# The first two batches with nine tokens per partition, and their scores ahead of V W_in, in a fused attention and two-layer kernel

## The chip, the cores and the metric

One core of a Trainium2 chip runs the whole program. The metric is the device time of one execution in microseconds, taken as the median of several runs; smaller is better. The engines are TensorE (PE, with its weight loads as PEld), VectorE (DVE), ScalarE (ACT), GpSimd (POOL) and SyncE (SP), which here issues nearly all transfers.

## What is computed

```python
# q, k, v: (8, 8, 576, 64)   phi: (8, 8, 576, 32)     batch, heads, tokens
a = np.exp(phi - phi.max(axis=2, keepdims=True))        # max over tokens
a = a / (a.sum(axis=2, keepdims=True) + 1e-9)
k_m = np.einsum('bhsm,bhsd->bhmd', a, k)                # 32 memories per head
v_m = np.einsum('bhsm,bhsd->bhmd', a, v)
scores = q @ k_m.transpose(0, 1, 3, 2) / np.sqrt(64)
attn = softmax(scores)                                  # with + 1e-9 under the sum
x = (attn @ v_m) -> (4608, 512)
h = x @ moe_w_in                                        # 512 x 2048
x = (h - np.tanh(h)) @ moe_w_out                        # 2048 x 512
h = np.maximum(np.maximum(x @ w1, x @ w2), x @ w3)      # 512 x 768 each
out = h @ moe2_w_out                                    # 768 x 512
```

The weights and all inputs arrive as the reference has them; `moe_w_in`, `moe_w_out` and the later weights come as 64-bit words, which the kernel turns into one or two 32-bit parts on chip (a conversion).

## The kernel before

Attention is not multiplied out: instead of attn @ v_m and then @ w_in, the kernel builds V W_in (the memories times the weights, `vw_gen`, PSUM tiles `ps_w`, SBUF tiles `vw`) per batch and half of the hidden columns, and multiplies the attention weights `at` by it (`ps_h`). Then follow tanh and subtraction (`emit_g`: `th` on ACT and DVE, `gh` in a high part by ACT and a low part by POOL), and the product with w_out (`emit_x`, PSUM tiles `ps_x`, weights `wo`). Every product of split numbers is three matmuls (`mm3`).

Work runs in steps: a step is one token tile times one block of 128 hidden columns. The first four tiles have 288 tokens each (half a batch); tiles 1 and 2 of the program are batch 0, tiles 3 and 4 batch 1. They go through `wo` blocks 0 to 3 first and through 4 to 7 after that. Later tiles have 256 to 512 tokens and all eight blocks at once. After two such phases the second layer runs from line 732 on.

For each batch `phi_gen` takes the maximum over tokens (`mx` on DVE, turned by PE into `ps_mx`, reduced to `mt`, spread by `dg`), subtracts and exponentiates; `kv_mm` multiplies by k and v (`ps_kv`), divides by the sums (`rc`, `n`) and turns the result (`ps_t`) into `kT` and `vT`. `q_gen` transposes the queries in blocks of 32 (`qT`), makes the scores (`sc`), transposes them back (`s`), takes the softmax, and transposes again (`aT`) into `at`, for each half `hf` of a batch.

In all batches tokens lie as 18 per partition of 32 partitions for the queries, and as four per partition of 128 plus a rest of 64 for phi, k and v. A query half of 4 heads takes 8 transfers (line 224), with 128-byte pieces.

A conversion (`conv`) is two ACT passes (`cvb`, `cva`) on a raw tile, three DVE passes on `cvb`, and a POOL addition; w_out needs another ACT cast and another POOL subtraction. There are three `raw` tiles, so a fourth fetch waits until one is converted.

Each engine works its instructions in program order. The order is that in which the Python code issues them, as rearranged by the scheduler of the language; the head of the program (lines 596 to 618) drives generators by hand, and later ones stand in three tracks: `fg` (attention of the next batches), `bg` (conversions) and `ld` (query loads), of which `slot` runs some pieces after every group of matmuls. `need` empties a track up to a named entry when a step wants what it makes.

Of the kernel before, what the change touches and what calls it, by code (L numbers as in the profile page):

```python
# [22 lines left out]
def kernel(  # L23
# [124 lines left out]
    def convs(*jobs, ahead=2):  # L148
        raws, k = [], 0
        for src, hi, lo in jobs:  # L150
# [7 lines left out]
            yield from conv(raws[k - 1], hi, lo)  # L158

    def conv(raw, hi, lo=None):  # L160
# [10 lines left out]
        live[0] -= 1  # L171
# [15 lines left out]
    def wi_conv(fq):  # L187
        t = wo1.tile([P, HP, FQ], F32, name="wi2") if fq == 2 else wi_p.tile([P, HP, FQ], F32, tag="wi", bufs=2, name="wi")
        yield from convs(*((moe_w_in[r * P:(r + 1) * P, fq * FQ:(fq + 1) * FQ], t[:, r], None) for r in range(HP)), ahead=2 if fq else 3)
        wi[fq] = t  # L190


    phi_t, kv_t, q_t = {}, {}, {}

# [99 lines left out]

    def kv_gen(b):
        yield from phi_gen(b)
# [5 lines left out]
    def q_gen(b, hfs):  # L302
        if 0 in hfs:
            ld.need(("q", b, 1))
# [4 lines left out]
        for hf in hfs:  # L309
            qT = []  # L310
            for g in range(2):
                t = ap.tile([P, 2, NH], F32, tag="qT", bufs=2, name="qT")
                V.transpose(out=t, in_=q_t[b, g][:, :, hf * JH:(hf + 1) * JH].rearrange("p r j d -> p r (j d)"))
                qT.append(t)
                yield
            scs = [bank(e, [P, NH], "sc") for e in range(2)]
            small([(scs[e][32 * r:32 * r + 32], kT[b][64 * e:64 * e + 64, r], qT[r // 2][64 * e:64 * e + 64, r % 2])
                   for r in range(HP) for e in range(2)])
# [26 lines left out]
            if hf:  # L345
# [25 lines left out]
    def wo_conv(fcs, p):  # L371
        ts = [p.tile([P, 2, DM], F32R, name=f"wo{fc}") for fc in fcs]
        for k, _ in enumerate(convs(*((moe_w_out[fc * P:(fc + 1) * P, :], t[:, 0], t[:, 1]) for fc, t in zip(fcs, ts)))):
            yield
        for fc, t in zip(fcs, ts):
            wo_t[fc] = t
# [49 lines left out]
    class Track:  # L426
# [6 lines left out]
        def step(self, now):  # L433
            if self.q and self.q[0][2] <= now:
                try:
# [3 lines left out]
                    self.step(now)  # L439

# [136 lines left out]
    G.memset(ones, 1.0)  # L577
    def drain(*gens):
# [17 lines left out]
    load_phi(0)  # L596
    load_kv(0)
    w0 = wi_conv(0)
    next(w0)
    drain(load_q(0, 0))  # L600
    next(w0)
    drain(load_q(0, 1))
    next(w0)
    drain(phi_gen(0))
    drain(kv_mm(0), w0)
    wo0 = wo_conv(range(4), wo_p)
    next(wo0)
    next(wo0)
    load_phi(1, fetch.last)
    load_kv(1, fetch.last)  # L610
    drain(q_gen(0, (0,)))
    drain(vw_gen(0, 0, 0))
    for _ in range(5):
        next(wo0)
    S.mark = at_cast[-1]
    background[0] = True
    drain(q_gen(0, (1,)), part_of(wo0, 6))
    background[0] = False
# [223 lines left out]
    def outs(g):  # L842
# [12 lines left out]
        def done(u):  # L855
            ob = get(f"ob{u % 2}")
            (S.copy if u % 2 else V.tensor_copy)(ob, ps[u])
            for r in range(0, P, 32):
                b, j = divmod((g * NG + u * P + r) // 32, TJ)
                dst = out[b * NS:(b + 1) * NS, :].rearrange("(p j) e -> j p e", j=TJ)  # L860
                DMA.dma_start(out=dst[j], in_=ob[r:r + 32, :])
# [66 lines left out]
```

## Time and profile before

| | us |
|---|---|
| median of 3 runs | 1371.06 |
| lowest, highest | 1369.17, 1372.64 |
| the profiled execution | 1365.75 |
| its span, first to last instruction | 1364.0 |
| PE busy | 1285.4 (94%) |
| PEld busy | 1157.4 (85%) |
| DVE busy | 751.2 (55%) |
| POOL busy | 531.8 (39%) |
| ACT busy | 507.1 (37%) |

Busy times are of one profiled execution. A busy share over the span is a mean over stages that differ; what counts is which engine is busy in the stage that is looked at. In the rows further down, "idle before <- releaser" says how long the engine stood and what ended it.

### The profile page before, as it was taken

The page shows a single profiled execution, that of the slowest core. Times are in us where ns is not written, and L with a number is a line of the kernel's source. Part 1 is how long each engine was busy: PE and PEld are TensorE (multiplying, and loading weights), DVE is VectorE, ACT ScalarE, POOL GpSimd, SP SyncE. Part 2 cuts the span into 40 slices and gives each one's busy share as a digit, 9 for nine tenths or more (in the row PEclk, how much of TensorE's full clock was granted, in tenths as well). Part 3 has the DMA queues.
Part 4 walks back from the last instruction along what each step waited for, and adds up shares of the span by engine and source line. Part 5 has one row for each costly group of instructions (what it writes and reads, how often), then busy time and mean ns, then how long its engine had stood idle before and what let it go on. Part 6 is the DMA issues. An engine that isn't in the chain of part 4 may idle for free.

```text
span 1364.0 us, 22739 instructions
## 1 busy us (share of the span) xinstructions
PE 1285.4 (94%) x8996; PEld 1157.4 (85%) x8996; DVE 751.2 (55%) x1189; ACT 507.1 (37%) x993; POOL 531.8 (39%) x470
## 2 busy tenths in 40 slices
PE   3578898999998999999999999999999999999998
PEld 1457696897897799898989999999999899999996
DVE  3868557666545755756643344555734546457342
ACT  2446244454334455555544332223322323233221
POOL 1637334554423546776754341132311312223110
PEclk9989998999999899999999999999999999999999
DMA  8874847866714536667575139838557477385431
GB/s 204 243 194 127 207 139 189 215 213 172 186 57 178 189 105 236 242 206 251 207 254 168 50 125 364 342 126 307 192 171 286 141 270 268 97 307 197 166 132 47
DMA packets 188394, 264.94 MB, mean 194 GB/s; under 512 B 94976, under 2 KB 160512, under 8 KB 179200
## 3 DMA queue, kind: packets, MB, share of 16 engines
q1 hardware_dynamic: 188000, 259.82, 58.3%
q0 software_dynamic: 288, 3.67, 0.7%
q8 instruction: 71, 1.16, 0.4%
q14 instruction: 35, 0.29, 0.1%
HBM read 199.49 MB, written 63.96 MB: 193 GB/s over the span
## 4 chain that ended last, share of the span: by engine, by line
PE 84%; DVE 7%; SPq 3%; issue 2%; POOL 2%; ACT 1%; DMA 1%; POOLq 0%; ACTq 0%; DVEq 0%
PE b L57 40%; PE ps_x L57 26%; PE ps_h L57 13%; PE ps_w L57 2%; PE ps_kv L57 2%; DVE cvb L57 2%; SPq L224 1%; DVE st L57 1%; DVE s L57 1%; POOL s L57 1%; DVE mx L57 1%; DMA raw<-in_moe_w_out_dram 1%; SPq L214 1%; DVE th L57 1%; DVE vw L57 0%
## 5 line engine op out<-in xcount | busy, mean ns | idle before, releaser
L57 PE MATMUL ps_x<-gh,wo 128*128 128x320 f32 (+2 forms) x2400 | 451.9, 335 | 7.2 <-DVE xo L57 5.5
L57 PEld LDWEIGHTS ps_x<-gh,wo 128*128 128x128 f32 x2400 | 381.4, 191 | 54.7 <-issue 22.9
L57 PE MATMUL b<-mv,sw 128*128 128x384 f32 x2268 | 401.6, 338 | 0.0
L57 PEld LDWEIGHTS b<-mv,sw 128*128 128x128 f32 x2268 | 399.1, 188 | 1.4 <-DMA sw<-sw_d 0.3
L57 POOL TENSOR_TENSOR gh<-th,gh 128x320 fp32r<-128x320 f32 (+2 forms) x200 | 209.8, 1051 | 259.0 <-ACT gh L57 248.9
L57 PE MATMUL ps_h<-at,vw 128*128 128x256 f32 (+2 forms) x1536 | 254.9, 307 | 20.4 <-DVE th L57 10.0
L57 PEld LDWEIGHTS ps_h<-at,vw 128*128 128x128 f32 x1536 | 227.7, 197 | 47.7 <-DVE th L57 15.6
L57 DVE TENSOR_TENSOR th<-ps_h,th 128x320 f32<-128x320 f32 (+2 forms) x200 | 106.7, 536 | 184.2 <-ACT th L57 183.5
L57 ACT ACTIVATE th<-ps_h 128x320 f32<-128x320 f32 (+2 forms) x200 | 95.2, 478 | 200.2 <-PE ps_h L57 185.7
L57 PE MATMUL b<-wz,mh 128*128 128x512 f32 x648 | 150.4, 390 | 1.1 <-DVE ob L57 1.1
L57 PEld LDWEIGHTS b<-wz,mh 128*128 128x128 f32 x648 | 121.3, 188 | 26.5 <-DVE ob L57 2.0
L57 ACT CAST gh<-th 128x320 fp32r<-128x320 f32 (+2 forms) x200 | 99.6, 499 | 96.0 <-DVE th L57 83.8
L57 POOL TENSOR_TENSOR c<-c,u 128x384 f32<-128x384 f32 x36 | 36.5, 1015 | 226.6 <-ACT u L57 226.6
L57 ACT COPY p<-b 128x384 f32<-128x384 f32 x108 | 51.8, 479 | 169.6 <-PE b L57 146.4
L57 DVE TENSOR_TENSOR c<-b,u 128x384 f32<-128x384 f32 x72 | 39.9, 554 | 97.0 <-PE b L57 97.0
L57 DVE TENSOR_SCALAR cvb<-cvb 128x512 f32<-128x512 f32 x112 | 69.8, 624 | 29.8 <-ACT cvb L57 27.0
L57 DVE TENSOR_TENSOR m<-c,m 128x768 f32<-128x768 f32 x72 | 69.0, 958 | 5.7 <-DVE c L57 0.9
L57 DVE TENSOR_TENSOR c<-b,p 128x384 f32<-128x384 f32 x72 | 37.7, 554 | 37.7 <-ACT p L57 34.2
L57 DVE TENSOR_TENSOR vw<-ps_w,vw 128x512 fp32r<-128x512 f32 x64 | 41.4, 681 | 22.9 <-ACT vw L57 22.9
L57 POOL TENSOR_TENSOR mv<-xr,mv 128x384 fp32r<-128x384 f32 x30 | 48.9, 1664 | 12.4 <-PE b L57 9.3
L57 POOL TENSOR_TENSOR m<-m,u 128x384 f32<-128x384 f32 x18 | 21.4, 1189 | 81.6 <-ACT u L57 80.2
L57 ACT CAST mh<-m 128x384 fp32r<-128x384 f32 (+1 forms) x54 | 31.8, 620 | 57.1 <-DVE m L57 57.1
(82 smaller groups left out, 1051.5 us busy)
## 6 DMA issues: line engine op xcount, KB each, us to landing
sw<-sw_d SPq DMA_DIRECT2D x52, 1792.0 KB, 7.6
sw_d<-so SPq DMA_DIRECT2D x9, 1792.0 KB, 7.1
raw<-in_moe_w_out_dram SPq DMA_DIRECT2D x22, 512.0 KB, 5.5
qt<-in_q_dram SPq DMA_DIRECT2D x128, 72.0 KB, 3.1
at_d<-at SPq DMA_DIRECT2D x16, 576.0 KB, 3.7
at<-at_d SPq DMA_DIRECT2D x8, 1152.0 KB, 6.3
raw<-in_moe_w_dram SPq DMA_DIRECT2D x18, 512.0 KB, 4.0
out_dram<-ob SPq DMA_DIRECT2D x144, 64.0 KB, 1.7
```

The source lines that it names most:

```text
L57: i = op(*a, **kw)
L214: DMA.dma_start(out=t[:64, i, :, 4], in_=x[b, :, 4 * P:].rearrange("h p d -> p h d"))
L224: q_dma.dma_start(out=t[64 * e + 32 * h:64 * e + 32 * h + 32, r], in_=src[e, h, r])
```

## The change

Batches 0 and 1 (`b < SPREAD`, with `SPREAD = 2`) get another layout. Partition p holds nine consecutive tokens; an upper and a lower set of 64 partitions hold odd and even heads, so a pair of heads fills 128 partitions. phi, k and v come in one transfer each, the queries of a batch in two, and the queries of both batches are issued at the start, into tiles that are used for other things later (`wo4`, `wo6`, `vw`). `kv_spread` replaces `phi_gen` and `kv_mm` for these batches: maxima and sums are trees of four DVE operations, the 40 one-column matmuls for the sums become two, and k and v take 72 matmuls of 64 rows. The query transposition covers all 576 tokens at once; the halves of a batch are then the upper and lower 32 partitions of each 64, so the scores of a half are two accumulating passes of 32 rows. `kT` is made in two parts to match (`kTs`). The output rows of these batches are written with stride 9.

The order changes as well. Scores of batch 0 stand ahead of V W_in; the second half of batch 0 moves from the head into the track `fg`, behind which `q_gen(1, (0,))` stands ahead of V W_in of batch 1; three w_in loads are issued early, the fourth into a `vw` buffer; a small exponential at the start loads ACT's table; `wo` blocks 4 to 7 are named as soon as each is converted, and `bg.until` runs the track only as far as the wanted block.

```diff
@@ small
-        ins = [T.matmul(o, w, x, start=True, stop=True).ins for o, w, x in mms]
+        ins = [T.matmul(o, w, x, start=not any(t), stop=not t or all(t), skip_group_check=bool(t)).ins for o, w, x, *t in mms]
@@ loads
+    def spread(t, x):
+        return DMA.dma_start(out=t.rearrange("p r j d -> p r (j d)"),
+                             in_=x.rearrange("(r e) n d -> r (e n) d", e=2).rearrange("r (p j) d -> p r (j d)", p=P)).ins
@@ kv_spread
+        mx = tree(V.tensor_max, pc, "mx")
...
+        for c in range(C9):
+            for r in range(HP):
+                for e in range(2):
+                    ins.append(T.matmul(ps[e][32 * r:32 * r + 32, :2 * D], ph[64 * e:64 * e + 64, r, c], t[64 * e:64 * e + 64, :, r, c], start=c == 0, stop=c == C9 - 1, skip_group_check=True).ins)
...
+        part = tree(V.tensor_add, pc, "part")
+        for e in range(2):
+            T.matmul(ps[e][:, 2 * D:], part[64 * e:64 * e + 64], ones[64 * e:64 * e + 64, :1], start=True, stop=True, skip_group_check=True)
@@ q_gen
+                w = [32 * (2 * e + hf) for e in range(2)]
+                small([(scs[e][32 * r:32 * r + 32].rearrange("p (j c) -> p j c", c=32), kT[b][w[e]:w[e] + 32, t, r], qT_s[b, r // 2][w[e]:w[e] + 32, r % 2, t], t)
+                       for t in range(2) for r in range(HP) for e in range(2)])
@@ emit_x
-        while 8 * ph + fc not in wo_t:
-            bg.need("wo")
+        bg.until(lambda: 8 * ph + fc in wo_t)
@@ start
+    S.activation(ap.tile([P, 2], F32, tag="mt", bufs=1, name="warm"), ones[:, :2], AF.Exp)
...
+    drain(kv_gen(0), part_of(w0, 3), part_of(q0, 2))
...
+    drain(q0, w0)
...
     drain(vw_gen(0, 0, 0))
...
+    fg.add(("q", 0, 0), q_gen(0, (1,)))
     fg.add("kv", kv_gen(1))
+    fg.add(("q", 0, 1, 0), q_gen(1, (0,)))
     fg.add(("vw", 0, 1, 0), vw_gen(0, 1, 0))
-    fg.add(("q", 0, 1, 0), q_gen(1, (0,)))
```

On SP, at the start of the program, the transfers stand like this before (`raw` is a tile of w_in or w_out, `qt` queries):

```order
L198 DMA phi<-in_phi_dram 128x8x128
L199 DMA phi<-in_phi_dram 64x8x32
L211 DMA kv<-in_k_dram 128x8x256
L214 DMA kv<-in_k_dram 64x8x64
L211 DMA kv<-in_v_dram 128x8x256
L214 DMA kv<-in_v_dram 64x8x64
L141 DMA raw<-in_moe_w_in_dram 128x1024
L224 DMA qt<-in_q_dram 32x18x32 x8
L141 DMA raw<-in_moe_w_in_dram 128x1024 x2
L224 DMA qt<-in_q_dram 32x18x32 x8
L141 DMA raw<-in_moe_w_in_dram 128x1024
L141 DMA raw<-in_moe_w_out_dram 128x1024
```

And now, where `qs` are the queries of batch 1:

```order
L211 DMA phi<-in_phi_dram 128x4x288
L211 DMA kv<-in_k_dram 128x4x576
L211 DMA kv<-in_v_dram 128x4x576
L142 DMA raw<-in_moe_w_in_dram 128x1024
L211 DMA qt<-in_q_dram 128x2x576 x2
L142 DMA raw<-in_moe_w_in_dram 128x1024 x3
L211 DMA qs<-in_q_dram 128x2x576 x2
L142 DMA raw<-in_moe_w_out_dram 128x1024
L211 DMA phi<-in_phi_dram 128x4x288
L211 DMA kv<-in_k_dram 128x4x576
L211 DMA kv<-in_v_dram 128x4x576
```

The 16 small query transfers between the w_in loads are gone, and batch 1's queries stand ahead of the first w_out.

On PE, from batch 1's `ps_t` to its first scores, before (the numbered `ps_x` are the four column blocks, `wo_305` to `wo_307` the blocks 1 to 3):

```order
L57 MATMUL ps_t<-ident,n 64x128 x4
L57 MATMUL ps_x_831<-gh,wo_305 128x288 x3
L57 MATMUL ps_x_828<-gh,wo_306 128x288 x3
...
L57 MATMUL ps_w<-wi,vT_90 32x512 x8
L57 MATMUL ps_x_828<-gh,wo_307 128x288 x2
L57 MATMUL ps_x_829<-gh,wo_307 128x288 x2
L57 MATMUL ps_x_830<-gh,wo_307 128x288 x2
L57 MATMUL ps_x_831<-gh,wo_307 128x288 x2
L57 MATMUL sc<-qT,kT 32x288 x16
```

And now (`wo_278`, `wo_279` are the blocks 0 and 1):

```order
L57 MATMUL ps_t<-ident,n 64x128 x2
L57 MATMUL ps_x_820<-gh,wo_278 128x288 x3
L57 MATMUL ps_x_821<-gh,wo_278 128x288 x3
L57 MATMUL ps_x_822<-gh,wo_278 128x288 x3
L57 MATMUL ps_x_820<-gh,wo_279 128x288 x2
L57 MATMUL ps_x_823<-gh,wo_278 128x288 x3
L57 MATMUL ps_x_820<-gh,wo_279 128x288
L57 MATMUL ps_x_821<-gh,wo_279 128x288 x3
L57 MATMUL ps_x_822<-gh,wo_279 128x288 x3
L57 MATMUL sc<-qT,kTs 32x288 x16
```

The scores stood behind `ps_w`, and stand ahead of it now, while the block that PE is at when `ps_t` comes is an earlier one.

On DVE, from the end of batch 0's second softmax to batch 1's `rc`, now (before, that softmax is over ahead of the first maxima of batch 1, and no `part` exists):

```order
L57 STREAM_TRANSPOSE aT<-s 128x576
L57 TENSOR_TENSOR th<-ps_h,th 128x288
L57 COPY dg<-mt 128x128
L57 STREAM_TRANSPOSE qT<-qs 128x1152 x2
L57 TENSOR_SCALAR cvb<-cvb 128x512
L57 TENSOR_TENSOR th<-ps_h,th 128x288
L57 TENSOR_TENSOR phi<-phi,ps_mx 128x1152
...
L57 TENSOR_SCALAR cvb<-cvb 128x512 x2
L57 SCALAR_TENSOR_TENSOR cvb<-raw,cvb 128x512
L57 TENSOR_SCALAR rc<-ps_kv 128x1 x2
```

The diagonal and the subtraction of batch 1 now stand behind the second softmax of batch 0 and behind both query transpositions.

## Rows read from the trace of the kernel before

**Rows 1.** Busy time by stage; columns as the first line says.
```profile
core 0: us, PE busy (x) PEld busy (x) DVE busy (x) ACT busy (x) POOL busy (x), PEclk, DMA share, GB/s
0.00:46.60 46.60, 14.47 (x220) 7.15 (x220) 22.50 (x42) 12.09 (x20) 10.64 (x15) 1.00 0.91 236
46.60:71.00 24.40, 18.80 (x89) 17.15 (x90) 21.71 (x31) 11.20 (x22) 16.47 (x13) 0.93 0.66 175
71.00:103.10 32.10, 22.26 (x306) 15.85 (x305) 21.82 (x42) 13.31 (x30) 12.15 (x12) 0.84 0.83 208
103.10:128.50 25.40, 20.74 (x150) 17.39 (x149) 23.90 (x34) 15.76 (x36) 21.36 (x19) 1.00 0.48 143
...
230.00:700.00 470.00, 460.65 (x3656) 401.46 (x3655) 281.32 (x466) 226.42 (x450) 257.24 (x226) 0.99 0.59 192
```

**Rows 2.** Instructions of the head: start, us, engine, operation, out<-in, count, idle before.
```profile
4.92 0.43 DVE L57 TENSOR_TENSOR mx<-phi 128x256 f32<-128x256 f32 x1 [3.91 <-DMA phi<-in_phi_dram]
...
9.90 1.49 DVE L57 TENSOR_TENSOR phi<-phi,ps_mx 128x1280 f32<-128x1280 f32 x1 [1.31 <-PE ps_mx L57]
...
11.46 1.28 ACT L57 ACT_TABLE_LOAD   x1 [11.46 <-DVE phi L57]
12.75 1.27 ACT L57 ACTIVATE phi<-phi 128x1280 f32<-128x1280 f32 x1
...
15.31 2.52 PE L57 MATMUL ps_kv<-kv,phi 128*32 128x128 f32 x40 [0.41 <-DMA kv<-in_v_dram]
...
18.24 0.89 DVE L57 TENSOR_SCALAR cvb<-cvb 128x512 f32<-128x512 f32 x2 [6.85 <-ACT cvb L57]
...
19.16 0.69 DVE L57 SCALAR_TENSOR_TENSOR cvb<-raw,cvb 128x512 uint32<-128x512 uint32 x1
20.00 1.26 POOL L57 TENSOR_TENSOR wi<-cvb,cva 128x512 uint32<-128x512 uint32 x1 [18.31 <-DVE cvb L57]
...
22.44 0.78 DVE L57 STREAM_TRANSPOSE qT<-qt 128x576 f32<-128x576 f32 x1 [2.59 <-DMA qt<-in_q_dram]
25.17 0.66 ACT L57 ACTIVATE cvb<-raw 128x512 f32<-128x512 f32 x1 [6.39 <-DMA raw<-in_moe_w_in_dram]
...
27.75 0.15 DVE L57 TENSOR_SCALAR rc<-ps_kv 128x2 f32<-128x2 f32 x1
...
37.05 0.83 DVE L57 STREAM_TRANSPOSE s<-sc 128x288 f32<-128x288 f32 x2
...
44.41 1.22 PE L57 MATMUL sc<-qT,kT 64*32 64x288 f32 x16 [4.42 <-DVE vw L57]
...
46.61 0.85 PE L57 MATMUL ps_h<-at,vw 128*128 128x288 f32 x2 [0.98 <-ACT at L57]
...
49.71 0.41 ACT L57 ACTIVATE th<-ps_h 128x288 f32<-128x288 f32 x1 [0.91 <-PE ps_h L57]
```

**Rows 3.** Transfers issued before 30 us (KB each, us to landing), and one stretch.
```profile
raw<-in_moe_w_in_dram SPq DMA_DIRECT2D x4, 512.0 KB, 5.2
qt<-in_q_dram SPq DMA_DIRECT2D x16, 72.0 KB, 4.3
...
kv<-in_v_dram SPq DMA_DIRECT2D x1, 1024.0 KB, 11.2
...
38.00:46.00 8.00, 3.18 (x32) 0.48 (x32) 6.10 (x12) 2.39 (x5) 4.03 (x3) 1.00 1.11 343
```

**Rows 4.** Instructions of batch 1's chain, and PE at batch 2's maxima.
```profile
60.37 3.88 DVE L57 TENSOR_TENSOR mx<-mx,phi 128x256 f32<-128x256 f32 x3
...
76.11 0.42 DVE L57 TENSOR_TENSOR n<-ps_kv,rc 128x256 f32<-128x256 f32 x1
...
86.42 0.72 PE L57 MATMUL sc<-qT,kT 64*32 64x288 f32 x16 [1.40 <-DVE vw L57]
...
94.13 0.78 DVE L57 STREAM_TRANSPOSE aT<-s 128x576 f32<-128x576 f32 x1 [1.35 <-POOL s L57]
...
127.40 0.41 PE L57 MATMUL ps_mx<-ident,mx 128*128 128x128 f32 x2 [1.41 <-DVE mx L57]
```

More of the change, by code (lines that the diff above doesn't have):

```diff
@@ L135, with fetch @@
     live = [0]
-    def fetch(src):
-        live[0] += 1
-        raw = cv_p.tile([P, 512, 2], U32, tag="raw", bufs=3, name="raw")
+    def fetch(src, room=None):
+        if room is None:
+            live[0] += 1
+        raw = room or cv_p.tile([P, 512, 2], U32, tag="raw", bufs=3, name="raw")
         u = src.bitcast(U32)
@@ L146, in held, with convs @@
         return cv_p.tile([P, 2, DM], F32R, tag="raw", bufs=3, name=name)
-    def convs(*jobs, ahead=2):
+    def convs(*jobs, ahead=2, done=None):
         raws, k = [], 0
@@ L158, in convs, with conv @@
             yield from conv(raws[k - 1], hi, lo)
-    def conv(raw, hi, lo=None):
+            if done:
+                done(k - 1)
+    def conv(raw, hi, lo=None, own=0):
         a = cv_p.tile([P, 512], U32, tag="cva", bufs=2, name="cva")
@@ L170, in conv @@
         V.scalar_tensor_tensor(out=b, in0=hw, scalar=0xC0000000, in1=b, op0=ALU.bitwise_and, op1=ALU.bitwise_or)
-        live[0] -= 1
+        live[0] -= 1 - own
         yield
@@ L188, in wi_conv @@
         t = wo1.tile([P, HP, FQ], F32, name="wi2") if fq == 2 else wi_p.tile([P, HP, FQ], F32, tag="wi", bufs=2, name="wi")
-        yield from convs(*((moe_w_in[r * P:(r + 1) * P, fq * FQ:(fq + 1) * FQ], t[:, r], None) for r in range(HP)), ahead=2 if fq else 3)
+        jobs = [(moe_w_in[r * P:(r + 1) * P, fq * FQ:(fq + 1) * FQ], t[:, r], None) for r in range(HP)]
+        if fq == 0:
+            raws = []
+            for r in range(HP):
+                raws.append(fetch(jobs[r][0], at_p.tile([P, 512, 2], U32, tag="vw", bufs=4, name="raw") if r == 3 else None))
+                yield
+            for x, (_, hi, lo) in zip(raws, jobs):
+                yield from conv(x, hi, lo, x is raws[3])
+        else:
+            yield from convs(*jobs)
@@ L295, in kv_gen @@
     def kv_gen(b):
+        if b < SPREAD:
+            yield from kv_spread(b)
+            return
         yield from phi_gen(b)
@@ L344, in q_gen @@
             DMA.dma_start(out=at_d[b][:, :, :, o], in_=f(at[:, :, :, o]))
-            if hf:
+            if hf and b + 1 >= SPREAD:
                 for g in range(2):
@@ L371, in wo_conv @@
     def wo_conv(fcs, p):
[L372 to L376, printed above, removed]
+        ts = []
+        for fc in fcs:
+            if fc < 4:
+                ts.append(p.tile([P, 2, DM], F32R, name=f"wo{fc}"))
+            else:
+                if fc % 2 == 0:
+                    pair = p.tile([P, 2, 2, DM], F32R, tag=f"wo{fc}", bufs=1, name=f"wo{fc}")
+                ts.append(pair[:, fc % 2])
+        yield from convs(*((moe_w_out[fc * P:(fc + 1) * P, :], t[:, 0], t[:, 1]) for fc, t in zip(fcs, ts)),
+                         done=lambda k: wo_t.__setitem__(fcs[k], ts[k]))
     wo_d = [dram.tile([P, 2, DM], F32, name=f"wo_d{fc}") for fc in range(FC)]
@@ L439, in step, with until @@
                     self.step(now)
+        def until(self, ready):
+            while not ready():
+                self.step(10 ** 9)
         def need(self, name):
```

156 lines of the change are left out of this document (127 added, 29 removed).

## The prediction

> **What bounds the kernel now.** I read the busy time by stage first. From 230 us on TensorE (PE) is busy 98% of the time (460.65 of 470 us), so work that ends earlier on another engine there is worth nothing. In the first 46.6 us PE is busy 14.47 us, from 71 to 103.1 us 22.26 of 32.10 us, while VectorE (DVE) is busy 21.71 of 24.40, 21.82 of 32.10 and 23.90 of 25.40 us in the three stages after the head [rows 1]. So the time can only change before some 130 us, and there by how early PE gets its first tiles and how long DVE, which all conversions and softmaxes pass through, holds up the rest. What PE does after that is the same work in both kernels, and moves as a block.
>
> Next I followed the head in order of time [rows 2]. phi is there at 4.92 us; its maximum, the subtraction (9.90), a table load of 1.28 us on ScalarE (ACT), the exponential (1.27) lead to ps_kv, which at 15.31 still waits for v. The sums of the products are read by DVE (rc) only at 27.75: DVE stands in order behind a conversion whose raw weights ACT got only at 25.17, after a wait of 6.39 us, because 8 query DMAs were issued ahead of them. The second set of queries then delays the score transposes to 37.05; the first ps_h runs at 46.61, the first tanh at 49.71.
>
> Last I read the transfers [rows 3]. A query DMA moves 72 KB and takes 4.3 us to land, a k or v of 1 MB 11.2 us, and w_in 5.2 us. From 0 to 46.6 us the queues carry 236 GB/s [rows 1], with large packets from 38 to 46 us 343 GB/s [rows 3].
>
> **Step 1, the loads.** SP now issues phi, k, v, one w_in, two query halves, three w_in, two query halves: 11 transfers, batch 1's queries among them, where 26 stood without these (the order of SP in the section on the change). I add their bytes, 0.59 for phi and each query half, 1.18 for k and for v, 0.52 for each w_in, from 2.2 us on at 343 GB/s, and put 1 us on for landing: v at 11.8 us (15.3 before), the first w_in 13.3, the queries of batch 0 at 15.0 and 16.7, the next two w_in at 18.3 and 19.8. At 236 GB/s the last of these comes at 27; both ends are kept. I take the high rate, because a packet is now 1,152 to 4,096 bytes, and that of the rows at 343 was of this kind.
>
> **Step 2, to the k and v products.** The tree of maxima is 4 DVE operations of 512, 256, 128 and 128 columns, where there were four of 256: 0.43 each [rows 2], so 1.7 us as before, from 4.92 to near 6.8 with the gaps. Half the transposing, the reduction and the diagonal go: of 3.1 us (6.8 to 9.90) about 2.1 remain. Subtraction and exponential have 1,152 columns in place of 1,280 (1.35 and 1.15 us), and the table load is done at the start. The exponential ends at 11.6 us, some 2.4 earlier, just as v lands. ps_kv is then 72 matmuls of 64 rows. 20 of them with 128 rows took 2.52 us, 0.126 each (40 instructions in [rows 2], since an fp32 matmul is two); in eight tiles at a time they could take half. So 4.5 to 9.1 us, end at 16.3 to 20.9. The 40 one-column matmuls are gone, for a tree of sums on DVE that lies beside the products; I cost their end at nothing, since PE's time here is covered by DVE's way to rc (step 3), and at 2 us of gain where ps_kv takes its long value.
>
> **Step 3, to the scores.** DVE does the sums (1.7), two conversion passes (0.89) after ACT's 0.66, a query transposition of twice 0.78 that waits for the queries (15.0 to 16.6), the third pass (0.69), then rc (0.15, twice), a reciprocal and n, 0.42 before and now in two halves [rows 4]: 1.2 in all, so 18.5 us. PE turns n in about 1.2. ACT stands on four conversion passes (0.66 each) whose last raw lands at 19.8, so the copy kTs ends at 21.5. If ps_kv takes the long value, the copy comes at 23.5; that is 2 us in the range. The scores are now 16 matmuls in place of 8 per half, since a head's 64 rows are split into two passes of 32. Eight took 1.22 us early (44.41) and 0.72 later (86.42) [rows 2, 4], PE's 1.2 and 2.4 GHz levels; so 2.4 us here and 0.7 extra in each of the three other halves.
>
> A rule weighed here: the Trainium skill, "TensorEngine Tiling (Array Packing)", section Performance Considerations, gives a contraction of 32 four row tiles, so the 16 could run at once for 1.2 us. The addresses speak against it: one half's scores use strips 32(2e+hf), two of the four. No row of before shows this form. By the page the first tiles come 1.2 us sooner.
>
> **Step 4, to the first tanh.** From the scores to the end of the transposition back (aT) an undisturbed half takes 86.42 to 94.91, 8.5 us [rows 4]. Here come 1.7 us for the longer, slower scores, and 2 us because two conversions (DVE 0.89 and 0.69, POOL 1.26 each, [rows 2]) stand in between and POOL multiplies only after them. aT ends at 33.7, ps_h starts near 35 when the last w_in is converted and V W_in cast, and the first tanh is at 38.4 in place of 49.71. **Head: 11.3 us earlier.**
>
> **Step 5, from the first tanh to batch 1.** Here the gain shrinks. Before, this stretch goes from 49.71 to the end of batch 1's first aT at 94.91, 45.2 us. DVE gets 4.7 us more work in it: half a conversion (0.8), the first part of batch 0's second softmax, which has moved behind the first ps_x steps (2.3), the sum tree (1.7), less one vw (0.68) and with four small operations (0.6). Against it, n to scores was 76.11 to 86.42 [rows 4], since PE had V W_in and ps_x ahead of them; the new PE order leaves 21 ps_x matmuls there, 3 to 4 us, so 6 us less. That would even be a gain of 1.6. But walking through the new DVE order with the durations above I meet three waits that were not there: the second softmax of batch 0 must end before the second tile's ps_h, and the diagonal and the subtraction of batch 1 stand behind it; two query transpositions of 1.5 stand ahead of that subtraction; and rc stands behind two conversions (3.2 us). The walk ends at 86.3 to 87, a stretch of 48.3 us. **Middle: 3.1 us given back.**
>
> DVE's operations are longer while POOL works: three maxima take 3.88 us at 60.37, where one took 0.43 [rows 2, 4]. In the trace before this is already in the stretch; for the added tree it makes 1.7 into up to 5 us, which I keep for the range. The Trainium skill says the same in "GPSIMD Engine Reference", section 1. Specifications: GpSimd's SBUF interfaces are shared with VectorE, with contention for instructions that have two SBUF inputs. By that rule the new trees, all two-input, are the dearest form here; the trace agrees (1.29 against 0.43 us), and the sum by it would be 3.3 us worse.
>
> **Step 6, to the end.** Batch 1's first tanh subtraction stands behind three of the seven DVE operations of the second half, not behind all: a transposition of 0.78, a reduction about as long and two short ones are spared, 2.0 us. One more conversion is left for this stretch, three operations at the mean of 0.70 that the stage from 103.1 to 128.5 us has with POOL beside it (23.90 us, 34 operations, [rows 1]): 2.1. The maxima of batch 2, for which PE waited 1.41 us [rows 4], now stand further back on PE: 1.4. **End: 1.3 us gained**; from there on PE is full and the lead stays. The out rows of batches 0 and 1 change their stride, not their number.
>
> **Sum.** −11.3 + 3.1 − 1.3 = −9.5 us. The profiled execution took 1365.75 us (span 1364.0), 5.3 under the median of the runs, 1371.06; the difference is taken over: 1361.5 us.
>
> **Rivals.** (a) *The loads stay slow*: with eleven transfers queued the rate is 236 GB/s, the third w_in lands at 27, and since ACT takes its passes in order kTs comes 7.5 us later. For it: the same queues gave that over the whole head. Against: the query packets were then 128 bytes. −9.5 + 7.5 = −2.0: 1369. (b) *DVE eats the lead*: at 21.71 of 24.40 us it is already the bound; with the trees at 5 us and the conversions stretched, the middle takes 54 us (8.8 more than before) and step 6 gains nothing: −2.5, 1368.5. (c) *Slower*: batch 0's second softmax, moved behind the first ps_x steps, runs on DVE and POOL together with the conversions of w_out 1 to 3 and batch 1's maxima. If its two-input operations take threefold, as the maxima at 60.37 did, the 15 of them grow from some 10 by up to 20 us; from 9.5 us of growth on the lead is gone, and PE, waiting twice, falls to its 1.2 GHz level after each wait as in the stretch from 71 to 103.1 us (granted 0.84, so 10 us at the lower level, up to 5 us lost [rows 1]). At half of the growth and one more such fall: −9.5 + 10 + 5 = +5.5, 1376.5. (d) *All of it is kept*: the walk's waits don't come, and that fall of 10 us is spared: −9.5 − 3.1 − 5 = −18, 1353.5.
>
> **Chances.** Forecast 0.60 (its own range 1356 to 1366), (a) 0.10, (b) 0.12, (c) 0.10, (d) 0.08. The range takes in (d) and (b) and leaves (c) out: 1353 to 1370.5. A measurement tells 0.3%, 4.1 us, from no change. Faster: the forecast and (d), 0.68; same: (a) and (b), 0.22; slower: (c), 0.10.
>
> **What would show it.** Right: v's wait before ps_kv ends near 12 us, kTs near 21.5, first tanh near 38, batch 1's first aT ending near 87, and busy times equal after 130 us less 9.5. Step 1 is wrong if ACT waits for raw beyond 21 us; step 2 if ps_kv takes over 7 us; step 5 if PE's waits before batch 1 are under 3 or over 12 us. All of it is wrong if PE has new idle time after 130 us.

## The result and the profile after

The changed kernel takes 1381.73 us (median of six runs, 1376.97 to 1384.28) against 1369.35 for the kernel before on the same chip: ratio 1.0091, 95% interval 1.0075 to 1.0107. It is 12.4 us slower, where 9.5 us less were forecast. The profiled execution took 1384.1 us (span 1382.3), 18.3 more than that of before; some 6 us of this lie in where the two profiled executions fall among their runs, and what follows is read by stage, not from the spans. Two executions of the run e15 below, of 1810 and 7014 us, are left out of its figures.

The stages of the first rows [rows 1], for the changed kernel:

```profile
core 0: us, PE busy (x) PEld busy (x) DVE busy (x) ACT busy (x) POOL busy (x), PEclk, DMA share, GB/s
0.00:46.60 46.60, 26.05 (x285) 15.39 (x286) 26.10 (x52) 17.28 (x32) 14.23 (x17) 1.00 0.76 281
46.60:71.00 24.40, 14.02 (x111) 12.21 (x117) 18.27 (x28) 7.23 (x14) 11.14 (x9) 0.66 0.22 70
71.00:103.10 32.10, 20.47 (x268) 15.72 (x251) 14.69 (x29) 9.34 (x20) 9.70 (x10) 0.71 0.66 178
103.10:128.50 25.40, 20.20 (x137) 14.92 (x130) 24.36 (x37) 15.59 (x33) 18.26 (x15) 0.95 0.70 177
```

In the first stage PE does 26.05 us in place of 14.47. In the second and third it does less than before, 34.49 against 41.06 us, at a granted clock of 0.66 and 0.71, mixtures of its 1.2 and 2.4 GHz levels, in place of 0.93 and 0.84; and DVE, which had 43.53 of 56.50 us to do there, has 32.96. So all engines stand more. From the first tanh to batch 1's first ps_h (39.66 to 103.28, before 49.71 to 95.67) PE is busy 40.86 of 63.62 us, before 32.42 of 45.96. The stretch is 17.7 us longer: 9.2 are waits, and for 8.4 PE is busy longer, with 416 matmul instructions in place of 357 and at a granted clock of 0.73 in place of 0.91. Over the whole span DVE and POOL are busy as long as before (751.8 and 531.9 us), PE 13.4 us longer (1298.8).

The head went as forecast (columns as in [rows 2]):

```profile
8.82 1.35 DVE L57 TENSOR_TENSOR phi<-phi,ps_mx 128x1152 f32<-128x1152 f32 x1 [0.89 <-PE ps_mx L57]
10.20 1.16 ACT L57 ACTIVATE phi<-phi 128x1152 f32<-128x1152 f32 x1 [7.96 <-DVE phi L57]
11.42 4.10 PE L57 MATMUL ps_kv<-kv,phi 64*32 64x128 f32 x144 [2.64 <-ACT phi L57]
...
19.18 0.66 ACT L57 ACTIVATE cvb<-raw 128x512 f32<-128x512 f32 x1 [1.50 <-DMA raw<-in_moe_w_in_dram]
20.29 0.36 ACT L57 COPY kTs<-ps_t 128x256 f32<-128x256 f32 x1
20.87 2.17 PE L57 MATMUL sc<-qT,kTs 32*32 32x288 f32 x32 [2.11 <-ACT vT L57]
32.77 0.77 DVE L57 STREAM_TRANSPOSE aT<-s 128x576 f32<-128x576 f32 x1
39.66 0.71 ACT L57 ACTIVATE th<-ps_h 128x288 f32<-128x288 f32 x2 [1.53 <-PE ps_h L57]
```

ps_kv no longer waits for v but for the exponential; the third raw of w_in, the last ahead of kTs, lands at 19.10 (the fourth at 20.23); kTs ends at 20.65, aT at 33.54, and the first tanh runs at 39.66, 10.05 us earlier than before.

Then PE's rows from 48 us to batch 1 (those with a wait, and the row behind the last):

```profile
48.74 1.32 PE L57 MATMUL ps_x<-gh,wo 128*128 128x288 f32 x8 [1.65 <-ACT wo L57]
52.67 3.25 PE L57 MATMUL ps_x<-gh,wo 128*128 128x288 f32 x12 [2.60 <-POOL wo L57]
...
59.62 0.85 PE L57 MATMUL ps_h<-at,vw 128*128 128x288 f32 x2 [2.53 <-ACT at L57]
61.11 4.19 PE L57 MATMUL ps_h<-at,vw 128*128 128x288 f32 x16 [0.64 <-POOL at L57]
...
67.08 1.06 PE L57 MATMUL ps_h<-at,vw 128*128 128x288 f32 x6 [1.56 <-DVE th L57]
69.54 4.40 PE L57 MATMUL ps_kv<-kv,phi 64*32 64x128 f32 x144 [1.39 <-ACT phi L57]
...
79.00 1.80 PE L57 MATMUL ps_t<-ident,n 128*32 128x128 f32 x20 [2.43 <-DVE n L57]
...
101.18 2.17 PE L57 MATMUL sc<-qT,kTs 32*32 32x288 f32 x32 [9.20 <-DVE vw L57]
103.28 3.00 PE L57 MATMUL ps_h<-at,vw 128*128 128x288 f32 x12
```

Eight waits, 22.0 us; with one of 0.75 us at 40.62 they are all of PE's idle time from the first tanh on. Batch 1's first ps_h is at 103.28; before it was at 95.67. The largest wait, 9.20 us, is put down to DVE. What DVE and ACT were doing, and what SyncE (SP) had issued:

```profile
96.42 0.82 DVE L57 COPY xo<-ps_x 128x288 f32<-128x288 f32 x2 [6.93 <-DMA xd<-xo]
...
96.39 0.40 ACT L57 COPY xo<-ps_x 128x288 f32<-128x288 f32 x1 [6.19 <-DMA xd<-xo]
...
79.84 0.62 SPq L261 DMA_DIRECT2D kv<-in_k_dram  x1
80.51 2.73 SPq L264 DMA_DIRECT2D kv<-in_k_dram  x1
83.28 0.73 SPq L261 DMA_DIRECT2D kv<-in_v_dram  x1
84.05 2.49 SPq L264 DMA_DIRECT2D kv<-in_v_dram  x1
86.66 12.00 SPq L700 DMA_DIRECT2D xd<-xo  x2
```

There is one xo buffer. The second tile's copies into it wait until the first tile's store has landed. That store is issued at 86.66, although its copies were done at 79.8, because batch 2's phi, k and v loads (2.9 MB) now stand ahead of it on SP; its data land after theirs (v at 93.68, the store at 96.30), 9.6 us from issue to landing. Behind the two copies stand batch 1's softmax and V W_in. Before, the store was issued at 72.21 and the loads from 75.71.

### The profile page after: what moved, and what is told of

The parts are those of the page before. It is cut to its first block, busy times and chain, and to the rows that moved or that the text cites. A ratio compares the mean times of both kernels' runs of the same rounds, so it can differ in the third digit from the quotient of the medians.

```text
span 1382.3 us, 22802 instructions
## 1 busy us (share of the span) xinstructions
PE 1298.8 (94%) x9058; PEld 1166.7 (84%) x9058; DVE 751.8 (54%) x1197; ACT 507.9 (37%) x994; POOL 531.9 (38%) x468
## 4 chain that ended last, share of the span: by engine, by line
PE 81%; DVE 7%; DMA 4%; SPq 2%; ACT 2%; issue 2%; POOL 2%; DVEq 0%; POOLq 0%; ACTq 0%
PE b L57 40%; PE ps_x L57 24%; PE ps_h L57 13%; DVE cvb L57 2%; PE ps_w L57 2%; PE ps_kv L57 2%; DMA raw<-in_moe_w_out_dram 1%; DMA raw<-in_moe_w_in_dram 1%; DMA xd<-xo 1%; DVE s L57 1%; DVE th L57 1%; DMA xo<-xd 1%; PE sc L57 1%; SPq L264 1%; DVE vw L57 1%
## 5 line engine op out<-in xcount | busy, mean ns | idle before, releaser
L57 PE MATMUL ps_x<-gh,wo 128*128 128x320 f32 (+2 forms) x2400 | 457.0, 338 | 12.3 <-DVE xo L57 7.8
L57 PEld LDWEIGHTS ps_x<-gh,wo 128*128 128x128 f32 x2400 | 385.6, 193 | 63.4 <-issue 28.0
L57 DVE TENSOR_SCALAR cvb<-cvb 128x512 f32<-128x512 f32 (+1 forms) x112 | 66.2, 595 | 21.2 <-ACT cvb L57 19.0
L57 PE MATMUL ps_w<-wi,vT 64*32 64x512 f32 x512 | 46.9, 661 | 14.8 <-DVE s L57 6.9
```

Of the source, the lines that this page charges most:

```text
L57: i = op(*a, **kw)
```

## The experiments

Times are medians, ratios are to the kernel before, on the same chip. The runs were measured in groups, each on a chip of its own, with medians of the kernel before from 1369.35 to 1370.36, so runs of different groups are best compared by their ratios. Two milestones go with them: batch 1's first ps_h and batch 2's first ps_kv (before 95.67 and 137.72; changed kernel 103.28 and 149.25). The expectations speak of the first run (e1), the third (e3), the run with both edits (e5) and of the one that began w_in later (e6, called the seventh experiment's kernel in e9 and e11).

**The store first (e1).** The two loads are taken out of kv_spread, emitted behind the first store and ordered after it, but for the two rests of k and v (128 KB each), which still go out just ahead of it (78.09 and 78.83). DVE, ACT, POOL and PE keep the changed kernel's order, row for row; only SP's differs.

```
-        if b == 1:
-            load_phi(b + 1)
-            load_kv(b + 1)
...
-            DMA.dma_start(out=xd[ph][:, :, o], in_=emit_x.xo)
+            store = DMA.dma_start(out=xd[ph][:, :, o], in_=emit_x.xo).ins
+            if not add and t0 == 0 and ph == 0:
+                load_phi(2, store)
+                load_kv(2, store)
```

> The changed kernel with one thing moved: SyncE issues the first tile's xd<-xo store ahead of batch 2's phi, k and v loads (about 2.9 MB) instead of behind them; every other engine's order is the changed kernel's. Theory T1 (the store behind those loads holds the only xo buffer, and DVE and ACT stop at the second tile's xo copies, 6.93 and 6.19 us, with PE idle 9.20 us before batch 1's first scores): the store is issued near 80 instead of 86.66 and lands within 3 us; the two waits fall under 1 us, PE's idle before the scores from 9.2 to about 3, and the time falls by 6 to 9 us, to about 1374. Rival T2 (what costs is batch 0's second softmax placed among the first ps_x steps, with PE's waits for w_out conversions and softmax steps, 12.8 us in eight waits between 48 and 80): the DVE queue is late anyway, another wait takes the place of the xo wait, and the time falls by no more than 2 us, to 1380 or more.

1373.95 us, ratio 1.0034 (1.0013 to 1.0055): 7.8 us less than the changed kernel. The store goes out at 79.57 and lands in 5.8 us (3 were expected), and PE's wait falls from 9.20 to 2.83 us:

```profile
94.28 1.44 PE L57 MATMUL sc<-qT,kTs 32*32 32x288 f32 x32 [2.83 <-DVE vw L57]
95.65 3.14 PE L57 MATMUL ps_h<-at,vw 128*128 128x288 f32 x12
```

One cause is shown: a store's place on SP's queue, 7.8 us. But batch 1's ps_h now comes when it did before, so the head's 10 us are still lost; batch 2's ps_kv is 3.7 us later than before (141.38), and the whole time 4.2 us longer. (The 12.8 us that T2 speaks of are seven waits, not eight.)

The same from the other side (e4), the kernel before with its store behind the loads:

```
+            if not add and t0 == 0 and ph == 0:
+                behind(store, load_kv.last)
```

> The kernel before with its first xd<-xo store made to follow batch 2's phi, k and v loads on SyncE, as in the changed kernel; part of the other orders shifts with it. T1: the wait appears here too: DVE and ACT stop 5 to 7 us at the second tile's xo copies, and the kernel is 4 to 9 us slower than before (ratio 1.003 to 1.007). T2: the kernel before has slack there, and the time stays within 2 us.

1373.16 us, ratio 1.0019 (0.9999 to 1.0039). The wait appears, on ACT as long as in the changed kernel, on DVE shorter:

```profile
91.68 0.82 DVE L57 COPY xo<-ps_x 128x288 f32<-128x288 f32 x2 [2.79 <-DMA xd<-xo]
...
91.73 0.70 ACT L57 COPY xo<-ps_x 128x288 f32<-128x288 f32 x2 [6.65 <-DMA xd<-xo]
```

It costs 2.6 us there by the ratio, 3.5 by the medians, less than T1 said and hardly told from nothing: before, batch 1's chain did not stand behind these copies to the same extent (ps_h 98.86, 3.2 later). The price of the store belongs to the new order around it.

**V W_in ahead of the scores again (e2).**

```
-    fg.add(("q", 0, 1, 0), q_gen(1, (0,)))
     fg.add(("vw", 0, 1, 0), vw_gen(0, 1, 0))
+    fg.add(("q", 0, 1, 0), q_gen(1, (0,)))
```

> The changed kernel with V W_in of batch 1 written ahead of batch 1's scores, as in the kernel before. The order that comes out also has the first xd<-xo store ahead of batch 2's loads, and five ps_x steps of batch 0 ahead of batch 1's ps_kv. T1 expects what e1 gives, 6 to 9 us less than the changed kernel, and nothing on top, since the scores were never late by V W_in. A rival T3 (scores put ahead of V W_in starve PE: the conversions that V W_in needs and the softmax run one after the other on DVE) expects more than e1: 10 us or more less, with PE's idle of 9.2 us gone. T2 expects at most 2 us less.

1377.24 us, 1.0058 (1.0038 to 1.0079): 4.5 us less than the changed kernel, but the store comes out first here too (69.92), which alone gave 7.8. Putting V W_in back ahead gains nothing, as far as a run tells that moves five ps_x steps as well; T3, which expected 10 us or more, falls.

**Batch 0's second half back in the head (e3).**

```
-    fg.add(("q", 0, 0), q_gen(0, (1,)))
+    background[0] = True
+    drain(q_gen(0, (1,)), part_of(wo0, 6))
+    background[0] = False
```

> The changed kernel with batch 0's second softmax half back in the head, beside the first w_out conversions, as in the kernel before; the xd<-xo store stays behind batch 2's loads. T1: the first tanh comes 6 to 9 us later, the waits of the second half between 59 and 69 go (6 us), the xo wait stays: the time changes by less than 3 us either way, 1379 to 1385. T2: the second half among the ps_x steps costs more than it gives (PE waits of 12.8 us between 48 and 80, at the lower clock), so the time falls by 5 to 10 us, to about 1374.

1373.44 us, 1.0017 (1.0001 to 1.0033): 8.3 us less by the medians, 10 by the ratios (1.0091 less 1.0017), as T2 said. The first tanh is at 41.91, only 2.25 later. Yet the xo wait is still in it, longer on DVE, and a wait of 7.97 us stands in front of it, from DVE's copies behind four conversions of w_in's second half (69.80 to 78):

```profile
78.65 4.46 PE L57 MATMUL ps_x<-gh,wo 128*128 128x288 f32 x21 [7.97 <-DVE xo L57]
```

So the half among the ps_x steps is a cause as well. With both undone (e5) the question was whether they add:

> The changed kernel with the edits of the first and the third run together: batch 0's second softmax half back in the head, and the first xd<-xo store ahead of batch 2's loads. The one took 7.8 us off the changed kernel, the other 10. If the two costs are separate (the store's wait, and the half among the ps_x steps) they add: about 1364 to 1366, ratio to the kernel before 0.996 to 0.998. If they are one cost seen twice (batch 1's softmax late behind the same DVE queue), the better of the two is all there is: 1370 to 1374.

1372.05 us, 1.0015 (1.0001 to 1.0028). They don't: it is the better of the two. PE still waits 7.98 us for DVE's xo copies at 78.04, DVE then waits 8.03 us for the store's landing (87.46), and batch 1's ps_h is at 97.37. What is won at one place is waited away at the next.

**Batch 0 alone in the new layout (e8)**, SPREAD = 1 and batch 1 loaded as before:

> The changed kernel with the nine-token layout for batch 0 alone: batch 1's phi, k, v and queries are loaded and worked as in the kernel before; batch 0's second half stays in the list behind the first steps. In the order that comes out the first xd<-xo store stands ahead of batch 2's loads. If the layout of batch 1 costs nothing by itself, the time is that of the first run, 1374 (1371 to 1377). If batch 1's layout costs (two full query turns of 1.3 us on DVE, two-pass scores, part behind exp), it is 3 us or more below, under 1371; if it gains (ps_kv, one turn for both halves), above 1377.

1376.35 us, 1.0050 (1.0033 to 1.0068), 2.4 us above the first run, with overlapping intervals. No cost of batch 1's layout by itself is seen.

**The conversions of w_in's second half.** The wait of 7.97 us pointed to their place on DVE, so they were begun later, from the sixth step, with both edits kept (e6):

```
-    fg.add(("vw", 0, 0, 1), chain(wi_conv(1), vw_gen(0, 0, 1)))
+    fg.add(("vw", 0, 0, 1), chain(wi_conv(1), vw_gen(0, 0, 1)), 5)
```

> As the run with both edits, and the second half of w_in's conversions (four, DVE, ACT and POOL) begun only from the sixth step on, so that they no longer stand ahead of rc, n and the first tile's xo copies on DVE. In the third run PE was idle 7.97 us from 70.67 on, waiting for DVE's xo copies behind four such conversions (69.80 to 77.95). Theory T4 (this idle is a cost of its own, of the order in which DVE took the conversions): it falls under 3 us, and the time is 4 to 6 us less than with both edits alone, about 1360. Rival: the conversions are only put off, V W_in's second half comes late, PE waits for it between 100 and 130, and the time stays within 2 us.

1368.50 us, 0.9995 (0.9978 to 1.0012). The wait is gone (0.39 us), batch 1's ps_h is at 87.61, 8.1 us before the old one. But batch 2's ps_kv is at 136.51, 1.2 us before, and the time is 3.5 us under both edits alone (2.7 by the ratios), less than T4's 4 to 6 (its "about 1360" doesn't go with these) and more than the rival's 2. From the fifth step on instead (e7):

> As the run before it, with w_in's second half begun from the fifth step on (two of the four conversions still ahead of rc). T4: between the two others, 2 to 4 us less than both edits alone. Rival: within 2 us of it.

1371.83 us, 1.0023 (1.0007 to 1.0039), no better than both edits alone.

**Is the lead lost to DVE's work or to PE's clock?** First DVE: 36 instructions of twelve conversions are left out in both kernels (e9, e10).

```
+        if not lean:
             V.tensor_scalar(f(b), f(b), TINY, HUGE, ALU.max, ALU.min)
             V.tensor_scalar(b, b, 3, 0x3FFFFFF8, ALU.logical_shift_left, ALU.bitwise_and)
...
             V.scalar_tensor_tensor(out=b, in0=hw, scalar=0xC0000000, in1=b, op0=ALU.bitwise_and, op1=ALU.bitwise_or)
```

> The seventh experiment's kernel (half in the head, store first, w_in from the sixth step) with the three VectorE instructions left out of each conversion of w_out's eight blocks and of w_in's second half (twelve conversions, 36 instructions, some 18 us of VectorE by 1.5 us each), so the values are not the reference's. It goes with the run below, the kernel before with the same left out. Open: the first tanh of this kernel comes 10 us earlier than before, batch 1's first ps_h 8 us earlier (87.6 against 95.7), and the whole time is the same (ratio 0.9995). Theory T5: the vector engines' conversions, the same in both kernels, pace the stretch from 88 to 150, so that PE's lead is waited away; then this kernel beats the one below by 6 to 10 us. Theory T6: PE's lead is lost to stretches at the lower clock after its waits, and these stay: then the two differ by 3 us or less.

> The kernel before with the same 36 VectorE instructions left out, so its values are not the reference's either. T5: faster than the kernel before by 0 to 4 us, and 6 to 10 us slower than the run above. T6: within 3 us of the run above.

(The first tanh of the kernel with w_in later is at 42.05, so 7.7 us early, not 10.) The pair took 1355.96 (0.9904, 0.9877 to 0.9930) and 1363.83 (0.9957, 0.9939 to 0.9975): 7.9 us apart, where with the conversions whole it was 0.9. (The new one has four timed executions. The kernel before gained 6.2 us by the medians, over the 0 to 4 that T5 gave it.) The stretch from the first tanh to batch 2's first ps_kv, columns as in the stages above; the kernel before:

```profile
49.71:137.72 88.01, 68.56 (x601) 57.28 (x600) 70.36 (x109) 42.56 (x91) 52.09 (x46) 0.92 0.63 170
```

the kernel with w_in later:

```profile
42.05:136.51 94.46, 76.47 (x653) 63.13 (x653) 70.34 (x122) 45.73 (x97) 52.18 (x47) 0.85 0.51 145
```

and the two without the 36 instructions, the new one first:

```profile
40.00:123.15 83.15, 70.38 (x633) 58.42 (x632) 48.83 (x85) 44.48 (x96) 49.27 (x46) 0.87 0.56 158
```

```profile
51.41:132.99 81.58, 67.01 (x615) 57.58 (x616) 44.22 (x81) 42.62 (x93) 46.93 (x46) 0.90 0.68 186
```

With some 70 us of DVE work in the stretch the new kernel needs 94 us where the old needs 88, and both end near 137. With 44 to 49 us both need 82 to 83, and the lead (11.4 us at the tanh, 9.8 at ps_kv) comes through to the end. So T5's forecast for the pair came true: with less for DVE to do, the head start is kept. How the conversions take it is not shown. By the rows above PE doesn't wait longer in the new kernel with the conversions whole (18.0 us idle against 19.5 before); it is busy 7.9 us longer, at a clock of 0.85 in place of 0.92. In its order 377 ps_h and ps_x matmuls stand ahead of batch 2's ps_kv, before 352. (24 such matmuls took 3.46 us at 74.37, so by an estimate these 25 are 3.6 us.) And without the three instructions a raw tile also becomes a weight sooner, so DVE's amount of work and the length of that way go together here.

Then the clock: 96 matmuls whose results nobody reads are put where PE waits, eight ahead of each of the first twelve ps_x steps, in e6 (e11) and in e1 (e12).

```
+        if i < 12:
+            for _ in range(8):
+                T.matmul(full[0][:, NH:], full[1][:, 0, 0, :P], full[2][:, 0, 0, :NT - NH], start=True, stop=True)
```

> The seventh experiment's kernel with eight matmuls of 224 columns, whose results nobody reads, ahead of each of the first twelve ps_x steps: 96 more matmuls, about 0.1 us each at 2.4 GHz, 10 us of PE work more, put where PE waits most. T6 (the lower clock after the waits eats the lead): the granted clock of 39 to 100, which was 0.66 to 0.70 in three of its stretches, comes up to 0.9 or more, and the time stays level or falls by up to 5 us although PE does more. T5: the clock may rise, but the time rises by 0 to 5 us, because the chain through DVE and POOL is what PE follows.

> The first experiment's kernel (the changed kernel with the store first) with the same 96 matmuls more. Its clock was 0.50 from 50 to 60 and from 70 to 80, 0.65 over 50 to 100. T6: the clock rises to 0.85 or more and the time falls by 3 to 8 us below the first run's 1374. T5: the time is the first run's or up to 5 us more, whatever the clock does.

1373.18 (1.0019, 1.0002 to 1.0036), 4.7 us more than its base (3.3 by the ratios), and 1373.61 (1.0023, 1.0005 to 1.0041), its base being 1373.95. In e11 the clock hardly rose (0.77 to 0.80 from 39 to 100), so it doesn't decide. In the second the clock did rise. The stretch 39 to 100 of the first run, and of that run with the matmuls:

```profile
39.00:100.00 61.00, 45.47 (x441) 36.98 (x441) 40.63 (x73) 23.59 (x49) 23.80 (x22) 0.69 0.46 136
```

```profile
39.00:100.00 61.00, 44.28 (x490) 35.77 (x489) 40.28 (x75) 24.02 (x49) 24.40 (x23) 0.86 0.49 140
```

0.69 to 0.86 of the clock, and the time is the same, though the matmuls themselves are some 10 us of PE work by the estimate above. In the first run's kernel the lower clock between these waits is not what holds the time, and T6 falls there. In e6, where the lead is lost, the clock as a part of the cause is not refuted.

**Order or amount on DVE?** With the conversions put by an order on DVE into its idle gap behind batch 1's n (e13), and with the first tiles' xo copies on ACT besides (e14):

```
-        V.tensor_scalar(f(b), f(b), TINY, HUGE, ALU.max, ALU.min)
+        c = V.tensor_scalar(f(b), f(b), TINY, HUGE, ALU.max, ALU.min)
+        if after:
+            behind(c.ins, after)
```

> As the run with both edits (1372.05), and the VectorE part of w_in's second half is ordered behind batch 1's n, by an order on VectorE alone, with no later step asked for: the conversions then stand in the gap that VectorE had from 71.2 to 77.8 in the run that began w_in later (idle 6.57 us there), behind rc, n and the first tile's xo copies. Theory T5a (the order on VectorE, not the amount, loses PE's lead: conversions ahead of rc, n and xo stop PE 8 us, conversions put off run into the busy stretch 91 to 126): PE keeps both the 8 us of batch 1's first ps_h and the stretch behind it, and the time is 1362 to 1366, ratio 0.994 to 0.997. T5b (the amount of VectorE work up to 130 us is what counts, wherever it stands): within 2 us of 1368.5, ratio 0.998 to 1.001.

> As the run beside it, and the xo copies of the first tiles (before step 32) all on ScalarE: eight copies of 0.41 to 0.46 us, some 3.5 us, off VectorE up to 130 us. T5a: the same as the run beside it within 1.5 us. T5b: 2 to 3 us less than it.

1369.41 (0.9995, 0.9983 to 1.0008) and 1367.35 (0.9978, 0.9964 to 0.9992), the lowest of the kernels that compute everything, and the only one of them whose interval lies wholly under 1: 2.8 us under the kernel before, 14 under the changed one. As the lowest of seventeen it may owe part of its 0.2% to chance. But neither could tell: the fourth block's raw load stood on SP behind batch 2's loads. The first of the two, ACT and then PE:

```profile
88.50 0.66 ACT L57 ACTIVATE cvb<-raw 128x512 f32<-128x512 f32 x1 [6.82 <-DMA raw<-in_moe_w_in_dram]
...
92.72 2.17 PE L57 MATMUL sc<-qT,kTs 32*32 32x288 f32 x32 [10.46 <-DVE vw L57]
```

So the loads went behind the second store (e15, e16):

> As e13, with batch 2's phi, k and v loads ordered behind the second xd<-xo store on SyncE instead of the first. In e13 the fourth w_in block's raw load, issued at 78.49, stood behind these loads; ScalarE waited for it 6.82 us (until 88.50), and with it batch 1's softmax, V W_in and PE (10.46 us before the second half's scores). If this is the same cause once more (what is wanted soon stands on SyncE's queue behind 2.9 MB that is wanted 40 us later), ScalarE's wait is under 1.5 us, PE's idle there falls under 4 us, batch 1's first ps_h comes at 86 to 89, and the time is 1361 to 1366 (ratio 0.993 to 0.997). If the amount of VectorE work up to 130 us decides (T5b), the wait goes but the time stays within 2 us of e13's 1369.4.

> As e15, with the first tiles' xo copies on ScalarE, as in e14. If the queue was the cause: 1359 to 1364, 1 to 2 us below e15, as e14 was 2 us below e13. If not: within 2 us of e14's 1367.4.

1368.62 (0.9986, 0.9972 to 1.0001) and 1370.85 (1.0001, 0.9987 to 1.0014). That wait is gone (0.66), but batch 1's ps_h is at 92.04, not 86 to 89, and the next wait is there: a w_out block's load, issued at 111.12 behind batch 2's sixteen query loads.

```profile
115.47 0.66 ACT L57 ACTIVATE cvb<-raw 128x512 f32<-128x512 f32 x1 [7.18 <-DMA raw<-in_moe_w_out_dram]
...
116.50 3.17 PE L57 MATMUL ps_x<-gh,wo 128*128 128x288 f32 x12 [5.66 <-ACT gh L57]
```

With these query loads issued by ACT (e17, e18):

> As e15, with batch 2's sixteen query loads issued by ScalarE instead of SyncE. In e15 the raw load of a w_out block, issued at 111.12, stood on SyncE behind them (issued one by one from 91.23 to 110.6), ScalarE waited 7.18 us for it and PE 5.66 us. If SyncE's queue was the whole of what held the lead back, no raw or xo wait over 2 us is left up to 130, and the time is 1361 to 1366 (ratio 0.993 to 0.997). If the amount of VectorE work decides (T5b), VectorE is busy over 90% from 95 to 120 and the time stays within 2 us of e15's 1369.

> As e17, with the first tiles' xo copies on ScalarE too. Queue the cause: 1360 to 1365, within 2 us of e17. VectorE's amount: 2 us or more below e17.

1371.40 (1.0008, 0.9993 to 1.0023) and 1370.74 (1.0005, 0.9991 to 1.0019). Now ACT stands at its own DMA issues; the profile of e17 names query loads as what released it:

```profile
93.45 6.81 ACTq L276 DMA_DIRECT2D qt<-in_q_dram  x5
100.30 0.59 ACT L57 CAST vw<-ps_w 128x512 fp32r<-128x512 f32 x1 [6.20 <-DMA qt<-in_q_dram]
```

Whether DVE's amount of work or the order in which its inputs come sets the floor stays open: no order that was tried was free of such a wait. T5b's own sign is missing: in e17 DVE is busy 16.05 of 25 us from 95 to 120, 64% where over 90% were expected, and the xo copies on ACT gave −2.1, +2.2 and −0.7 us in the three pairs. In these six kernels batch 1's ps_h came from 90.35 to 95.95 and batch 2's ps_kv from 132.95 to 138.88, the one without regard to the other: the earliest ps_h (e18) has its ps_kv at 137.61, the earliest ps_kv (e14) follows a ps_h at 94.03.

**What the whole time follows.** This is read from the traces and was not tested by a run. Take 1 us for each us that batch 2's first ps_kv comes after 137.72: for all twenty kernels this gives the measured difference to the kernel before to within −1.2 and +3.0 us. Batch 1's first ps_h gives no such thing: e2 and e13 have it at 95.75 and 95.95, and 1.0058 and 0.9995. The rows behind that ps_kv suggest why. It reads the only phi and kv tiles, so batch 3's loads into them follow it on SP (from 141.94 before, from 140.48 in e6), then eleven query loads, and only then the load of the partial sums (`xo<-xd`) that DVE adds to and PE waits for. The kernel before:

```profile
161.56 0.63 SPq L547 DMA_DIRECT2D xo<-xd  x1
...
166.84 1.06 PE L57 MATMUL ps_x<-gh,wo 128*128 128x288 f32 x3 [4.88 <-DVE xo L57]
```

and e6:

```profile
159.59 0.63 SPq L683 DMA_DIRECT2D xo<-xd  x1
...
165.02 1.09 PE L57 MATMUL ps_x<-gh,wo 128*128 128x288 f32 x3 [7.43 <-DVE xo L57]
```

Counted in ps_h and ps_x matmuls, PE of e6 comes to this wait 5.6 us ahead (the 450th starts at 151.72, before at 157.36) and leaves it 1.8 us ahead. At a ps_w at 217.26 (before 218.10), behind a wait of ACT for a raw of w_out (5.74 us, before 2.86), 0.8 us are left. In the pair without the 36 instructions the load is issued 8.7 us apart (147.95 and 156.63), and 8.5 us are left at that ps_w. So a lead on PE alone is waited away there, and one that SP's queue has too is kept.

## Why the prediction was wrong

**Steps 1 to 4 held.** v landed at 10.85 (11.8 said), the third raw of w_in at 19.10 (19.8), ps_kv 4.10 us (4.5 to 9.1; so a 64-row pass costs under half a 128-row one here), kTs 20.65 (21.5), scores 2.17 (2.4), aT 33.54 (33.7), first tanh 39.66 (38.4). The head is 10.05 us earlier, 11.3 were forecast. The scores took the time of two passes over two strips, not the 1.2 us that the rule of four row tiles would have given (the Trainium skill, "TensorEngine Tiling (Array Packing)", section Performance Considerations): with two of the four strips in use the trace follows the addresses. They ran at the lower clock, as the step said: the traces of the two kernels record no granted clock that early (none before 56.8 and 44.4 us), but in e6 the same scores take the same 2.17 us at a granted 0.50. The rate of 343 GB/s was not one of large packets alone (975 of its 3,180 packets were under 512 bytes); the new loads ran at some 390. Two sums of the prediction are loose and carry nothing: 4.7 against 6 us is a gain of 1.3, not 1.6, and (d) adds to −17.6, not −18.

**Step 5 failed.** 48.3 us were forecast for the stretch to the end of batch 1's first aT, 60.9 measured (39.66 to 100.55), so 15.7 us given back instead of 3.1. The walk went along DVE, POOL and PE with durations from the trace, and left SP out after the head: it named the three waits of batch 1's chain but not that batch 2's loads now come ahead of the first xd store on the queue, which goes out 14 us later than before, and that the one xo buffer ties DVE and ACT to its landing. This was the term at nothing in the sum, worth 7.8 us: of the 12.6 us that the step missed, 7.0 go with it (e1 has 53.9 us for this stretch). The rest goes when, besides, the half is back in the head and w_in's second half is converted later (e6: 44.8 us). The Trainium skill's rule on GpSimd and VectorE ("GPSIMD Engine Reference", section 1. Specifications) agrees with the rows in a small way: the added tree's last operation took 1.25 us in e1, where POOL worked beside it (71.80 to 73.13), and 0.29 in e3, where POOL stood. It is not where the time went. One-input conversions, which the prediction leaves out here, were long beside POOL too: two took 1.82 us at 46.50, and 0.89 at 44.97.

The forecast's own sign for this step was PE waits over 12 us before batch 1: they were 22.8. It was a weak sign, since the kernel before has 13.5 us of them in its own stretch.

**Step 6 failed too.** "From there on PE is full and the lead stays" is refuted by the kernel with w_in later: 8.1 us of lead at batch 1, 1.2 at batch 2's ps_kv, 0.9 at the end. It rested on PE's busy share after 230 us, and its rows leave out 128.5 to 230, where PE of the kernel before waits 11.2 us. The pair without the 36 instructions shows that the conversions decide whether the lead is kept; by the count of matmuls PE itself is still 5.6 us ahead at 152 us and loses this in the waits before 166 and 218.

**The rivals.** (c) was the right side: its place, batch 0's second softmax among the w_out conversions, is measured at 8 to 10 us. Its mechanism, two-input operations growing threefold and PE's clock falling, is not shown: the subtraction in it did take 1.83 us where it took 0.76 undisturbed, but all 22 two-input operations of DVE from 44 to 80 us were together some 6 us over the shortest rows of their forms, where 10 to 20 were put for 15 of them, and lifting the clock in e1's kernel gave nothing. (b), DVE eats the lead, describes what is left when the new waits are taken out, 1368.5 us forecast for it and 1368.50 measured in that kernel; the exact meeting is chance, since it was worked out as a longer middle. The chance of 0.10 for slower was too small because each of the three moved pieces (the half, the conversions, batch 2's loads) was costed on one queue only.

## What to carry to other kernels

When a generator moves, every DMA it issues moves on the issuing queue too: write out that queue up to the next point where a buffer is waited for, as one does for the compute engines, and ask of each transfer when its data are wanted against what stands behind it. A head start of TensorE is worth what the engines and queues that feed it can keep up with: before counting it, shorten their work in both versions and see whether the lead comes through, and look for the row that the whole time follows (here batch 2's first ps_kv, not batch 1's first ps_h). A buffer with one copy turns a late store into a stop of two compute engines.

## What the runs showed of the hardware

A store of 0.59 MB took 9.6 us to land with 2.9 MB issued just ahead of it, 5.8 us with most of these loads behind it (e1), 3.3 us with no other transfer (issued at 98.10 in the changed kernel). ACT, made to issue sixteen small loads, stood 6.20 us while five of them were issued: moving transfers to a compute engine's queue moved the wait into that engine. The granted clock of a stretch could be lifted from 0.69 to 0.86 by matmuls that nobody reads, with no gain in a kernel whose PE had waits for other engines.
